# Down products of a SwiGLU layer by a two-by-two scheme with seven products, on one Trainium2 core

## Chip, core and metric

The kernel runs on one core of one Trainium2 chip. The metric is the time of the whole program on the device in microseconds; the time before is the median of three runs. One further run was profiled; its span is the time between the first and the last recorded instruction. TensorE is PE, VectorE DVE, ScalarE ACT, GpSimd POOL; SyncE (SP) issues nearly all transfers.

## What is computed

One transformer block on 2048 tokens of width 640 in f32: layer norm, attention with 32 heads of width 20, a projection and a residual sum, then layer norm, a SwiGLU layer of inner width 1728, and a residual sum. The change touches the last two lines.

```python
h = x + _A_ref(_layernorm(x), A_wqkv, A_wo)
def _B_ref(x, w_gate, w_up, w_down):
    g = _silu(x @ w_gate)
    u = x @ w_up
    return (g * u) @ w_down
h2 = h + _B_ref(_layernorm(h), B_w_gate, B_w_up, B_w_down)
```

## The kernel before

Every f32 product is made of three matmuls in the type fp32r: each operand is split into a high part (a copy, mostly on ACT) and a low part (the operand less its high part, on DVE or POOL; `split`, L75 to L77), and high by high, high by low and low by high are summed in PSUM.

**Attention.** Tokens come in four chunks of 512 (`CH`), 16 tiles of 128. After the projections for queries, keys and values, 32 units `u` (eight groups of four heads by four chunks) run over 16 key tiles `kt` each. `ORDER` spells the order in a key tile: scores (`s`, `S`), the maxima for coming units (`m`, `M`; `next_max`, `max_one`, L177 to L183), and once (`W`) the weighting of the values. When the last maximum of a unit is made, `max_all` (L187) reduces them on DVE and makes two small POOL instructions (L194, L195); two key tiles later `max_finish` (L199) transposes them on PE (L202). When a unit's sums are complete, ACT copies them out (L846).

**Weight preparation.** At `W`, one task of `prepare_weights` (L661) may be issued, except in unit 0, in key tiles 3 and 4, and where `max_all` just was (L927, L928). A block `f` of 128 inner columns (14 blocks, the last of 64) has the tasks load, nothing, two of sums, and eight that make one piece each; a piece is copied and subtracted on POOL (L676, L677) into a staging tile, of which there are four, and stored by the next task (L669) into `w_d`. Then `rows` (L740) does the same for the down weights, two blocks at a time: load, nothing, and four pieces (block by half of the 640 columns) into `d_d`. The tasks have to be through by unit 24, where the loads of `wo` begin.

**Feed-forward.** The chunks are taken in two pairs, `ELEMENTS` (L794) lists (pair, block) with the short block 13 first, and `e` is the place in this list. For a full block, `blocks` (L1103) makes gate and up for both chunks with seven products of 6 matmuls (128 x 512) and four of 3, in eight steps; what `done(0)` and `done(1)` receive, after steps' work 5 and 7, is the block's gated value for one chunk. For block 13 `plain` (L1082) has six steps. The PSUM banks `ps_a` (four) hold these products and `ps_b` (four) the down products. Weights come through rings (`Ring`, L771): eight places for units, three for lasts, four for halves of the down weights; `fill` loads the next ones at each step.

`parts` (L1029) splits the gated value. `to_come` (L1058) makes 16 pieces of it, each one `down` (L1039): for one token tile and one half, three matmuls of 128 x 320 (L1047; two in block 13, whose high and low parts share the rows) and one DVE addition to `h` (L1052). A block's pieces are issued in the next element's steps, so PE has them between its wide products. After block 12, the last of a pair, `out` is stored.

**Late tokens.** Pair 0 is normed and transposed before the feed-forward; pair 1 (chunks 2 and 3) during its first elements, by `late_tokens` (L1200): 15 small DVE items (`soon`, five a step), then 21 items (`late`, one a step), five for each token tile: for each of the two chunks a norm (L1216) and transposes on PE (L1232), split into the tile `kept` (two buffers) and stored into `z_d`; the sums of four blocks on POOL (L1249); and these split and stored into `t_d` (`store`, L1206). At e = 13 and 14 `swap` loads `z_d` and `t_d` over pair 0's operands (`SWAPS`, L1281). `step` (L1289) does all this in order: fills, swaps, down pieces, then a late item.

Of the kernel before, what the change touches and what calls it, by code (L numbers as in the profile page):

```python
# [43 lines left out]
def tile_block(ctx: ExitStack, tc: tile.TileContext, x, wqkv, wo, wg, wu, wd, out):  # L44
# [13 lines left out]
    d_d = [dram.tile([P, 2, 2 * HALF], F32R, name=f"d_d{f}") for f in range(NF)]  # L58
# [504 lines left out]
    wo_hi = pc.tile([P, ND, D], F32R, name="wo_hi", bufs=1)  # L563
    wo_lo = pc.tile([P, ND, D], F32R, name="wo_lo", bufs=1)
# [95 lines left out]

    def prepare_weights():  # L661
# [20 lines left out]
        def block(f):  # L682
# [33 lines left out]
            def unit(kind):  # L716
                store()
                t = staged([P, 2, 2, P])
                part(src[kind], t[:, 0], t[:, 1])
                stores.append((w_d[f][:, UNITS.index(kind)], t.rearrange("p i k n -> p (i k n)")))  # L720

            def last():
                store()
                t = staged([P, 2, 2, P])
# [7 lines left out]
            if not whole:  # L732
                return [load, nothing] + [lambda k=k: unit(k) for k in ("A11", "A12")] + [last]
            return (
                [load, nothing, lambda: sums(0), lambda: sums(1)]
# [4 lines left out]
        def rows(fs):  # L740

            raw = {}

            def load():
                store()
                for f in fs:
# [9 lines left out]
            def half(f, i):  # L756
                store()
                t = staged([P, 2, HALF])
                part(raw[f][:, i * HALF : (i + 1) * HALF], t[:, 0], t[:, 1])
                stores.append((d_d[f][:, i], t.rearrange("p i n -> p (i n)")))  # L760

            return [load, nothing] + [lambda f=f, i=i: half(f, i) for f in fs for i in range(2)]
# [4 lines left out]
        for f in range(0, NF, 2):  # L767
            tasks += rows((f, f + 1))
# [135 lines left out]
    for u in range(NU):  # L904
# [4 lines left out]
        for kt in range(NT):  # L909
# [49 lines left out]
            if kt in (12, 13) and 0 <= k + kt - 12 < ND:  # L959
                assert not preparing  # L960
                load_wo(k + kt - 12)
# [17 lines left out]
    for c in range(2, NC):  # L979
        h_c[c] = pe2.tile([P, TPC, D], F32, name=f"h{c}")  # L980
# [48 lines left out]
    def parts(f, s):  # L1029

        y_hi = pd2.tile([P, CH], F32R, name="y_hi", bufs=3)
        if f < NF - 1:
            y_lo = pd2.tile([P, CH], F32R, name="y_lo", bufs=3)
            split(s, y_hi, y_lo, nc.gpsimd)
            return y_hi, y_lo
        split(s[:LASTW], y_hi[:LASTW], y_hi[LASTW:], nc.gpsimd)
        return y_hi, None

    def down(c, t, half, d, y_hi, y_lo, final):  # L1039
        tt = c * TPC + t  # L1040
        pairs = [(y_hi, d[:, 0]), (y_hi, d[:, 1])]
        if y_lo is not None:
            pairs.append((y_lo, d[:, 0]))
        hs = slice(half * HALF, (half + 1) * HALF)
        ps = ps_b()
        for n, (a, b) in enumerate(pairs):
            nc.tensor.matmul(  # L1047
                ps[:, :HALF], a[:, t * P : (t + 1) * P], b,
                start=(n == 0), stop=(n == len(pairs) - 1),
            )  # L1050
        h = h_c[c][:, t, hs]
        nc.vector.tensor_tensor(out=h, in0=ps[:, :HALF], in1=h, op=ALU.add)  # L1052
        if final and half == 1:
            nc.sync.dma_start(out[tt * P : (tt + 1) * P, :], h_c[c][:, t, :])

    pending = []

    def to_come(pair, ys, final):  # L1058

        d = []  # L1060
        for i in range(2):
            for t in range(TPC):
                for half in range(2):
                    def piece(i=i, t=t, half=half):
                        if len(d) < 2:
# [282 lines left out]
```

## Time and profile before

| | |
|---|---|
| runs | 2137.73, 2142.70, 2144.39 us; median 2142.7 |
| profiled run | 2144.3 us; its span 2142.5 us |
| granted TensorE clock | 0.994 of full speed on the mean |
| DMA | 270.32 MB, mean 126 GB/s |
| down matmuls (L1047) | 896 + 416, DVE additions (L1052) 448 |
| loads | 186 units, 26 lasts, 56 halves |

A row of a timeline has the start and the length in us, engine, line, operation and operands; what stands in brackets is the idle time ahead of it and what ended that. A row of waits has the total, the times and the longest. Rows of the DMA queue have packets, MB and the share of the 16 engines' time in the stretch. Rows of the chain have start, length, and the number of instructions that were merged.

### The profile page before, as it was taken

How to read it: one execution, taken by the hardware profiler on the slowest of the kernel's cores; microseconds unless marked ns; L12 is line 12 of the kernel's file. 1: busy time of each engine (PE TensorE's matmuls, PEld its weight loads, DVE VectorE, ACT ScalarE, POOL GpSimd, SP SyncE). 2: the span in 40 equal slices, each digit the busy share in tenths (PEclk: the TensorE clock that was granted, in tenths of full speed). 3: DMA queues.
4: the chain of work that ended last, by engine and by line, in shares of the span. 5: the costliest groups of instructions: out<-in, count | busy, mean ns of one | idle time of the engine just before them, and what ended most of it. 6: DMA issues, size and time to landing. Idle time of an engine off the chain costs nothing.

```text
span 2142.5 us, 35011 instructions
## 1 busy us (share of the span) xinstructions
PE 2100.7 (98%) x12726; PEld 1224.7 (57%) x12726; DVE 1758.3 (82%) x2929; ACT 1281.1 (60%) x2491; POOL 495.0 (23%) x633
## 2 busy tenths in 40 slices
PE   7999999999999999999999999999999999999998
PEld 5766775333333333333333333335588888888887
DVE  6999996999889998999999999996367766666666
ACT  4222216999889998999999999996733211111111
POOL 5222212334343342410000010001145311111111
PEclk9999999999999999999999999999999999999999
DMA  7565532442533535522102113130238644764443
GB/s 249 158 189 172 159 107 81 120 150 94 161 115 104 172 100 154 185 92 56 48 22 77 30 46 92 26 109 22 71 112 256 211 133 146 276 228 145 131 143 108
DMA packets 203316, 270.32 MB, mean 126 GB/s; under 512 B 45624, under 2 KB 97848, under 8 KB 203144
## 3 DMA queue, kind: packets, MB, share of 16 engines
q1 hardware_dynamic: 189560, 241.86, 36.1%
q10 hardware_dynamic: 13584, 26.23, 4.0%
q8 instruction: 101, 1.65, 0.3%
q14 instruction: 71, 0.58, 0.1%
HBM read 182.68 MB, written 84.54 MB: 125 GB/s over the span
## 4 chain that ended last, share of the span: by engine, by line
PE 87%; DVE 6%; DMA 3%; POOL 2%; issue 2%; ACT 1%; SPq 0%; ACTq 0%; POOLq 0%; DVEq 0%
PE acc L836 23%; PE ps_a L993 14%; PE ps_max L177 14%; PE ps_one L826 14%; PE ps_b L1047 8%; PE ps_one L418 5%; DVE mx L171 3%; PE ps_one L452 2%; PE ps_wide L167 2%; PE ps_max L608 2%; PE ps_b L608 1%; DMA t_d<-kept 1%; DVE mx L183 1%; POOL zz L1249 0%; PE ps_one L386 0%
## 5 line engine op out<-in xcount | busy, mean ns | idle before, releaser
L832 ACT ACTIVATE probs<-ps_one 128x512 f32<-128x512 f32 x2048 | 1045.2, 621 | 137.0 <-PE ps_one L826 132.3
L183 DVE TENSOR_REDUCE mx<-ps_max 128x1 f32<-128x512 f32 x1632 | 1021.5, 683 | 108.2 <-PE ps_max L177 59.4
L826 PE MATMUL ps_one<-q_stk,k_stk 62*128 62x512 f32 x2048 | 552.2, 423 | 1.7 <-ACT probs L832 1.0
L836 PE MATMUL acc<-probs,v_stk 128*32 128x512 f32 x4096 | 547.9, 607 | 0.3
L177 PE MATMUL ps_max<-k_stk,q_stk 60*128 60x512 f32 x1632 | 544.1, 462 | 2.4 <-DVE mx L183 1.5
L177 PEld LDWEIGHTS ps_max<-k_stk,q_stk 60*128 60x128 f32 x1632 | 231.6, 185 | 431.7 <-DVE mx L183 411.3
L826 PEld LDWEIGHTS ps_one<-q_stk,k_stk 62*128 62x128 f32 x2048 | 300.7, 186 | 81.0 <-ACT probs L832 51.7
L171 DVE TENSOR_REDUCE mx<-ps_wide 128x2 f32<-128x1024 f32 x208 | 240.7, 1217 | 13.9 <-PE ps_wide L167 13.5
L1107 DVE TENSOR_TENSOR tmp<-ps_a,tmp 128x512 f32<-128x512 f32 x208 | 141.2, 689 | 125.7 <-PE ps_a L993 124.0
L1052 DVE TENSOR_TENSOR h<-ps_b,h 128x320 f32<-128x320 f32 x448 | 197.5, 483 | 11.5 <-PE ps_b L1047 11.5
L1047 PE MATMUL ps_b<-halves,y_hi 128*128 128x320 f32 x896 | 197.6, 309 | 0.2 <-DVE h L1052 0.2
L836 PEld LDWEIGHTS acc<-probs,v_stk 128*32 128x32 f32 x4096 | 80.9, 108 | 161.4 <-issue 152.7
L76 ACT ACTIVATE y_hi<-tmp 128x512 fp32r<-128x512 f32 (+1 forms) x56 | 35.3, 632 | 228.6 <-DVE tmp L1108 225.3
L1047 PEld LDWEIGHTS ps_b<-halves,y_hi 128*128 128x128 f32 x896 | 156.8, 188 | 20.7 <-DVE h L1052 2.0
L993 PE MATMUL ps_a<-t,units 128*128 128x512 f32 x624 | 162.8, 396 | 0.2 <-DVE kept L77 0.2
L77 POOL TENSOR_TENSOR y_lo<-tmp,y_hi 128x512 fp32r<-128x512 f32 x52 | 67.9, 1305 | 386.1 <-PE ps_a L993 241.9
L993 PE MATMUL ps_a<-z,units 128*128 128x512 f32 x516 | 133.7, 394 | 0.0
L1047 PE MATMUL ps_b<-halves,y_lo 128*128 128x320 f32 x416 | 127.5, 307 | 0.3 <-POOL y_lo L77 0.3
L993 PEld LDWEIGHTS ps_a<-t,units 128*128 128x128 f32 x624 | 112.5, 188 | 19.0 <-DVE kept L77 0.4
L194 POOL CAST both<-neg 128x16 fp32r<-128x16 f32 x32 | 6.6, 208 | 465.4 <-DVE neg L190 236.8
L993 PEld LDWEIGHTS ps_a<-z,units 128*128 128x128 f32 x516 | 93.1, 187 | 15.8
L993 PE MATMUL ps_a<-z,lasts 128*128 128x512 f32 x324 | 92.5, 393 | 0.2 <-DVE kept L77 0.2
(140 smaller groups left out, 1763.3 us busy)
## 6 DMA issues: line engine op xcount, KB each, us to landing
units<-w_d SPq DMA_DIRECT2D x186, 256.0 KB
w_d<-staged SPq DMA_DIRECT2D x106, 256.0 KB
halves<-d_d SPq DMA_DIRECT2D x56, 320.0 KB
raw<-qk_d SPq DMA_DIRECT2D x70, 160.0 KB
k_stk<-qk_d SPq DMA_DIRECT2D x64, 160.0 KB
q_stk<-qk_d SPq DMA_DIRECT2D x64, 160.0 KB
d_d<-staged SPq DMA_DIRECT2D x28, 320.0 KB
rb<-r_d SPq DMA_DIRECT2D x32, 256.0 KB
```

The costliest lines, as they stand in the source:

```text
L77: lo_engine.tensor_tensor(out=lo, in0=src, in1=hi.bitcast(F32), op=ALU.subtract)
L171: nc.vector.tensor_reduce(mx[:, :, pair, t, kc], ps, axis=AX.X, op=ALU.max)
L177: nc.tensor.matmul(ps, queries[u][rows, pair, t * P : (t + 1) * P], keys[u // NC][rows, pair, kc * CH : (kc + 1) * CH], start=True, stop=True,
L183: nc.vector.tensor_reduce(mxs[u][:, b, pair, t, kc : kc + 1], ps, axis=AX.X, op=ALU.max)
L418: nc.tensor.matmul(ps, w[:, k, m * P : (m + 1) * P], a[:, k, :], start=(n == 0 and k == 0), stop=(n == 2 and k == ND - 1),)
L826: nc.tensor.matmul(ps, keys[u // NC][rows, p, kt * P : (kt + 1) * P], queries[u][rows, p, :], start=True, stop=True,)
L832: nc.scalar.activation(probs[p][:, b, :], ps, AF.Exp, scale=scale)
L836: nc.tensor.matmul(acc[32 * j : 32 * j + 32, :], values[u // NC][:, kt, j * VW : j * VW + 32], probs[j // 2][:, j % 2, :], start=(kt == 0) ...
L993: nc.tensor.matmul(ps, w[k][:, i], z[k][:, j], start=(first and m == 0), stop=(last and m == len(n) - 1),)
L1047: nc.tensor.matmul(ps[:, :HALF], a[:, t * P : (t + 1) * P], b, start=(n == 0), stop=(n == len(pairs) - 1),)
L1052: nc.vector.tensor_tensor(out=h, in0=ps[:, :HALF], in1=h, op=ALU.add)
L1107: add = lambda out, ps, x: nc.vector.tensor_tensor(out=out, in0=ps, in1=x, op=ALU.add)
```

## The change

The down products of two neighbouring blocks (the inner dimension, 2 x 128) and two neighbouring token tiles (2 x 128), by the two halves of the 640 columns, are made with seven products for eight. The scheme needs four sums of the gated values (in a group, on POOL, `prepare`), four of the down weights (in the preparation, now stored as seven pieces in `j_d`), and sums of the products: three products are added to `h` directly, four into sums of their own, which `put_together` adds to `h` at a pair's end with eight POOL additions a group. Couples are joined in pair 0 for blocks 0 to 11, in pair 1 for 0 to 9; the others (`own`) go as before, in groups of two token tiles with four pieces.

The sums take the place of chunks 2 and 3 of `h`, which are stored to `h_d` in the late tokens and come back into the places of chunks 0 and 1 after pair 0's output (`bring_back`). The operands `yp` take the place of the late tokens' tiles: a joined group can only be prepared when `late` is through (`opened`); it has 17 items now, four for each token tile. `RATES` says how many pieces an element issues. The ring of halves has nine places. The gated value goes into a tile `y` (seven buffers). The preparation has ten staging places, two tiles of five, in the places of `wo_hi` and `wo_lo` (which are allocated later now), and one `nothing` more after each load. Of `soon`, seven items go with a step.

```diff
-        def staged(shape):
+        def staged(n):
             count[0] += 1
-            return pc.tile(shape, F32R, name="staged", tag=("o_hi", "o_lo")[count[0] % 2])
+            t = stages[count[0] % 2][:, count[0] // 2 % 5, : 2 * n]
+            return t.rearrange("p (i n) -> p i n", i=2), t
...
+            tasks = [load, nothing, nothing]
+            if together:
+                tasks += [lambda: sums(0), lambda: sums(1)]
+                for i, (_, name, _) in enumerate(SEVEN):
+                    tasks.append(lambda i=i, n=name: piece(n, j_d[fs[0] // 2][:, i]))
+            else:
+                for f in fs:
+                    for i in range(2):
+                        tasks.append(lambda f=f, i=i: piece((f, i), d_d[f - NF + 4][:, i]))
...
+    SEVEN = (
+        ("A11", "B11", 0), ("S2", "T2", 1), ("S3", "T3", 2), ("S1", "T1", 3),
+        ("A12", "B21", (0, 0)), ("S4", "B22", (0, 1)), ("A22", "T4", (1, 0)),
+    )
+    def own(pair, f):
+        return f >= (NF - 2, NF - 4)[pair]
...
+        def prepare(self):
+            if self.parts is not None or not (pools or self.fs[0] == NF - 1):
+                return
...
+            p = self.parts = pools[0].tile([P, 2, 7, P], F32R, name="yp", tag="yp", bufs=3)
...
+            a, b = self.ys
+            split(cols(b, t, 2), p[:, 0, 1:3], p[:, 1, 1:3], nc.gpsimd)
+            x = tmp().rearrange("p (k n) -> p k n", k=4)
+            a11, a21, a12 = cols(a, t)[:, 0], cols(a, t + 1)[:, 0], cols(b, t)[:, 0]
+            tt = nc.gpsimd.tensor_tensor
+            tt(out=x[:, 0], in0=a21, in1=cols(b, t + 1)[:, 0], op=ALU.add)
+            tt(out=x[:, 1], in0=x[:, 0], in1=a11, op=ALU.subtract)
+            tt(out=x[:, 2], in0=a11, in1=a21, op=ALU.subtract)
+            tt(out=x[:, 3], in0=a12, in1=x[:, 1], op=ALU.subtract)
+            split(cols(a, t), p[:, 0, :1], p[:, 1, :1], nc.gpsimd)
+            split(x, p[:, 0, 3:], p[:, 1, 3:], nc.gpsimd)
...
+        def seven(self, n):
+            name, _, place = SEVEN[n]
+            if self.tp == 0:
+                self.d.append(down_ring.take())
+            d, k = self.d[n], SLOTS.index(name)
+            y_hi, y_lo = self.parts[:, 0, k], self.parts[:, 1, k]
+            ps = self.multiply([(y_hi, d[:, 0]), (y_hi, d[:, 1]), (y_lo, d[:, 0])])
+            if self.tp == 3:
+                down_ring.free()
+            if isinstance(place, tuple):
+                self.add(ps, *place)
+            else:
+                own_sum = sums[self.tp][place]
+                if self.fs[0] == 0:
+                    nc.vector.tensor_copy(own_sum, ps)
+                else:
+                    nc.vector.tensor_tensor(out=own_sum, in0=ps, in1=own_sum, op=ALU.add)
+            if n == 6 and own(self.pair, self.fs[1] + 1):
+                self.put_together()
...
+    def prepare_some():
+        for g in waiting[:2]:
+            g.prepare()
...
             z = zs[c, t] = pl.tile([P, D], F32, name="z3", bufs=2)
...
+            stores.append((h_d[c - 2, :, t], h_c[c][:, t, :]))
...
-            items.append(lambda t=t: keep_sums(0, t))
-            items.append(lambda t=t: (store(), keep_sums(1, t)))
+            items.append(lambda t=t: (keep_sums(0, t), keep_sums(1, t)))
...
+    RATES = {
+        1: (6, 2), 2: (10, 0), 3: (4, 7), 4: (17, 0), 14: (12, 0), 15: (16, 0), 16: (16, 0),
+        25: (18, 0), 26: (22, 0), 27: (26, 0),
+    }
...
+    def bring_back():
+        for c, t in again:
+            nc.sync.dma_start(h_c[c][:, t, :], h_d[c, :, t])
+            h_c[c + 2] = h_c[c]
+        again[:] = stored
+        stored.clear()
...
+        number, begin = RATES.get(e, (14 if e else 0, 0))
+        each = spread_over(number, steps, begin)
...
             for _ in range(each[n]):
-                if old:
-                    old.pop(0)()
+                next_down()
+            if not late and e > 2:
+                prepare_some()
+            for _ in range(2):
+                if chores:
+                    chores.pop(0)[2]()
...
             elif late:
                 late.pop(0)()
+                if not late:
+                    pl_ctx.close()
+                    opened()
```

More of the change, by code (lines that the diff above doesn't have):

```diff
@@ L732, in block @@
             if not whole:
-                return [load, nothing] + [lambda k=k: unit(k) for k in ("A11", "A12")] + [last]
+                return [load, nothing, nothing] + [lambda k=k: unit(k) for k in ("A11", "A12")] + [last]
             return (
-                [load, nothing, lambda: sums(0), lambda: sums(1)]
+                [load, nothing, nothing, lambda: sums(0), lambda: sums(1)]
                 + [lambda k=k: unit(k) for k in ("A11", "A12")] + [last]
@@ L1027, in quarter_sums @@
         ]
[L1029 to L1065, printed above, removed]
-                            d.append(down_ring.take())
-                        down(2 * pair + i, t, half, d[half], *ys[i], final)
-                        if (i, t) == (1, TPC - 1):
-                            down_ring.free()
-                    pending.append(piece)
+    def own(pair, f):
+        return f >= (NF - 2, NF - 4)[pair]
@@ L1072, in bank, with next_down, to_come @@
+    def prepare_some():
+        for g in waiting[:2]:
+            g.prepare()
+    def next_down():
+        if not waiting:
+            return
+        g = waiting[0]
+        prepare_some()
+        f, i = g.steps.pop(0)
+        f(i)
+        if not g.steps:
+            waiting.pop(0)
+    def to_come(i, pair, fs, ys, d):
+        waiting.extend(Group(pair, tp, fs, ys, d) for tp in (2 * i, 2 * i + 1))
     def bank():
@@ L1317, in tile_block @@
             (plain if f == NF - 1 else blocks)(step, done)
-        to_come(pair, ys, f == NF - 2)
-    for f in pending:
-        f()
+        before = ys
+    while waiting:
+        next_down()
 _INS = ["A_x", "A_wqkv", "A_wo", "B_w_gate", "B_w_up", "B_w_down"]
```

186 lines of the change are left out of this document (149 added, 37 removed).

## The prediction

> **What bounds the kernel now.** I read the busy shares on the profile's page first, then the busy times by stretch, then the chain that ended last.
>
> ```profile
> PE 2100.7 (98%) x12726; PEld 1224.7 (57%) x12726; DVE 1758.3 (82%) x2929; ACT 1281.1 (60%) x2491; POOL 495.0 (23%) x633
> ```
> ```profile
> 1600.00:1700.00 100.00, 97.52 (x516) 83.78 (x516) 74.76 (x155) 29.88 (x58) 47.13 (x43) 1.00 0.77 237
> 1700.00:1800.00 100.00, 100.00 (x522) 87.45 (x521) 68.00 (x134) 15.66 (x25) 12.98 (x10) 1.00 0.43 141
> ```
>
> The columns of a stretch are PE, PEld, DVE, ACT and POOL busy, granted clock, DMA share and GB/s. From 1670 us on, PE never rests until the tail, the other engines have room, and DMA is under half used: there, a matmul less is its time less. Between 1600 and 1670 PE loses 2.5 us and DMA is at 0.77 and more; that stretch decides this case.
>
> The chain between 1700 and 1800 us is PE alone and gives the price of a matmul:
>
> ```profile
> 1707.59 1.39 PE ps_a L993 x6
> 1708.98 0.88 PE ps_b L1047 x6
> ...
> 1712.13 2.09 PE ps_a L993 x9
> ...
> 1727.14 1.39 PE ps_a L993 x6
> ```
>
> Six down matmuls take 0.875 us, 0.146 each; a 512-wide one takes 0.2325 (2.09 / 9). One block of 54 wide and 48 down matmuls takes 19.55 us (1727.14 - 1707.59).
>
> **The change, part by part.** The profiled run is 2144.3 us, its span 2142.5; the median of the runs is 2142.7, 1.6 below the profiled run. I work on the span.
>
> *1. Matmuls removed.* Pair 0 joins f = 0 to 11 (6 couples), pair 1 f = 0 to 9 (5). Each couple has 4 groups of two token tiles, each group 7 products for 8, each product 3 matmuls: 11 x 4 x 3 = 132 matmuls of 0.146 us: **-19.3 us**, if PE stays full. DVE has 28 adds for 32 in a couple, and no new kind but a copy: nothing.
>
> *2. Weight preparation.* Before: 13 x 12 + 5 + 7 x 6 + 1 = 204 tasks, one for a key tile at most. After: 13 x 13 + 6 + 6 x 12 + 2 x 7 + 1 = 262; it ends some 4.5 units later, still ahead of the loads of wo. PE mostly does not feel these tasks, but three times it does:
>
> ```profile
> 453.44 0.62 ACT L846 ACTIVATE o<-acc 128x512 f32<-128x512 f32 x1
> ...
> 562.70 0.61 ACT L846 ACTIVATE o<-acc 128x512 f32<-128x512 f32 x1
> 600.72 0.63 ACT L846 ACTIVATE o<-acc 128x512 f32<-128x512 f32 x1
> ...
> 680.18 0.62 ACT L846 ACTIVATE o<-acc 128x512 f32<-128x512 f32 x1
> ...
> 789.25 0.62 ACT L846 ACTIVATE o<-acc 128x512 f32<-128x512 f32 x1
> ...
> 902.09 0.62 ACT L846 ACTIVATE o<-acc 128x512 f32<-128x512 f32 x1
> ```
> ```profile
> PE ps_one L202 <- POOL both L195: 7.6, 3, 4.1
> ```
> ```profile
> 611.89 0.42 SPq L696 DMA_DIRECT2D raw<-in_B_w_gate  x1
> ```
> ```profile
> 621.01 0.72 POOL L708 TENSOR_TENSOR sums<-raw 128x256 f32<-128x256 f32 x1 [21.20 <-DMA raw<-in_B_w_up]
> ```
> ```profile
> 610.00:640.00 30.00, 25.82 (x168) 0.89 0.40 124
> ```
>
> L846 ends a unit; from 453.44 to 562.70, to 680.18, to 789.25 and to 902.09 it is three units each: 109.3, 117.5, 109.1 and 112.8 us. The second and fourth are 8.2 and 3.7 long: **11.9 us** lost. The mechanism: POOL, in order, stands at L708 until a load lands 9 us after its issue; behind it wait the small casts of max_all (L194, L195), and for these the transposes of max_finish, so PE sits for 7.6 us in three waits, and its clock falls for a while (0.89). Counting the tasks against the units, these are just the three units where max_all follows the first task that needs a load (sums(0), or the first half) within a key tile. After the change each load has one key tile more (36.4 / 16 = 2.3 us), and that task falls within one key tile of max_all only at units 3, 4 and 19. Of these only unit 4 has its load issued late, three key tiles ahead (6.8 us), like the mildest of today's three, whose unit (562.70 to 600.72, 38.0 us) is 1.6 us over a third of 109.3; I leave it 2 us. Ten staging places take POOL's waits for stores away too. I take **-10 us**, with ends 0 (the stalls come back elsewhere) and -12. The Trainium skill, "TensorE: Matmul & The Clock Gate", Part 1, says that an idle window of about 3.4 us halves PE's clock until it has been busy as long; the 4.1 us wait with 0.89 after it agrees, and by that rule an idle PE costs more than its idle time, which speaks against part 3 below.
>
> *3. The late tokens.* This is what the change puts at risk. late_tokens writes chunks 2 and 3 out; its 17 items now have to be through by step 3 of e = 3, where pl closes, and a joined group can't be prepared before. What they store goes up by h_d, and what PE has to do meanwhile goes down: steps of e = 1 to 3 issue 6, 10 and 4 down pieces, 16 of them of two matmuls, and the rest of the down work comes later.
>
> ```profile
> 1602.77 1.56 PE L993 MATMUL ps_a<-z,units 128*128 128x512 f32 x6
> ...
> 1624.28 0.71 PE L1232 MATMUL ps_a<-ident,z 128*128 128x128 f32 x5
> 1624.74 1.65 PE L993 MATMUL ps_a<-t,units 128*128 128x512 f32 x6
> ```
> ```profile
> q1 hardware_dynamic: 14691, 28.11, 42.8%
> ```
> ```profile
> q1 hardware_dynamic: 15567, 11.33, 94.9%
> ...
> units<-w_d SPq DMA_DIRECT2D x13, 256.0 KB
> z_d<-kept SPq DMA_DIRECT2D x6, 512.0 KB
> t_d<-kept SPq DMA_DIRECT2D x4, 512.0 KB
> halves<-d_d SPq DMA_DIRECT2D x4, 320.0 KB
> z_d<-kept SPq DMA_DIRECT2D x6, 128.0 KB
> lasts<-w_d SPq DMA_DIRECT2D x1, 256.0 KB
> ```
> ```profile
> 1631.69 0.64 ACT L76 ACTIVATE kept<-zz 128x512 fp32r<-128x512 f32 x1 [4.53 <-DMA t_d<-kept]
> ```
> ```profile
> 1626.39 0.53 SPq L1206 DMA_DIRECT2D t_d<-kept  x1
> ...
> 1670.91 0.53 SPq L1206 DMA_DIRECT2D t_d<-kept  x1
> ```
>
> PE alone would need 3 x 54 x 0.2325 + 32 x 0.146 + 8 flips x 0.46 = 46 us from 1602.8, and stand at the first joined piece at 1649. DMA needs longer. From 1900 to 2100 us the queue moved 28.11 MB of loads at a share of 42.8%, thus 328 GB/s when at work. From 1630 to 1670 it was at 94.9%; its loads (4.98 MB) take 15.2 of these 38.0 us at that rate, which leaves 22.8 us for 6.03 MB of z_d and t_d: 264 GB/s. After the change there must pass from 1603 on: z_d and t_d 9.43 MB, 35.7 us; h_d eight of 0.328 MB, 8.0; nine halves, filled at once, 9.0; 19 units and 3 lasts, 17.6: **70 us**, until 1673. The stores are in the way of the engines: kept has two buffers, ACT waits for a store before it writes the next (the row of 4.53 us), and behind it wait the copies and Silus that free PE's banks. The last three of the four token tiles take 14.8 us each today (1626.39 to 1670.91, the first t_d of each), in five items, nearly all of it DMA; with four items a tile moves as many bytes (h_d in place of a unit and the halves), so it takes no less. I put the first joined piece at 1678: 1673 and 5 us for the last landing and the operands.
>
> ```profile
> 1670.00:1680.00 10.00, 10.00 (x53) 8.51 (x52) 7.70 (x15) 2.39 (x4) 3.67 (x3) 1.00 0.89 269
> ```
>
> PE is full from 1670, so its third block ends two blocks ahead of 1707.59, at 1668.5, and by then 32 more full pieces are done, 32 x 0.4375 = 14.0 us. So the stretch costs 1678 - 1668.5 + 14.0 = **+23.5 us**. The ends: -5.5 (PE alone, 1649) and +30 (a few us of DMA idle in the first 20).
>
> *4. Operands of the joined groups.* For each group POOL does one subtraction of 256 columns, one of 128, one of 512 and four additions of 128.
>
> ```profile
> 723.59 0.73 POOL L677 TENSOR_TENSOR staged<-raw,staged 128x256 fp32r<-128x256 f32 x1
> ...
> 724.63 0.46 POOL L677 TENSOR_TENSOR staged<-raw,staged 128x128 fp32r<-128x128 f32 x1
> ...
> 823.07 0.88 POOL L677 TENSOR_TENSOR staged<-raw,staged 128x320 fp32r<-128x320 f32 x1
> ...
> 1619.54 1.29 POOL L77 TENSOR_TENSOR y_lo<-tmp,y_hi 128x512 fp32r<-128x512 f32 x1 [1.41 <-ACT y_hi L76]
> ```
>
> 0.73 + 5 x 0.46 + 1.29 = 4.3 us; 44 groups, 190 us in some 440. They are made a group ahead, four steps or some 9 us, which hides them; ACT waits inside for POOL, 2.6 us (0.73 + 4 x 0.46), with p1's copy behind it on ACT and DVE's adds behind that, and PE's four banks cover it. I take 0; without the cover each group would wait a part of it, at 0.5 us 44 x 0.5 = **22 us**. The 64 put_together additions of 0.88 us run two a step on POOL: 1.8 us of a step of 2.4, with the operands beside them in e = 14: 0 to +3. The store of out waits for them on SP, and behind it the ring loads, eight units ahead: nothing.
>
> *5. More loads.* 89 halves come in for 56; eight h_d loads come at e = 15 and 16. At e = 13 they meet the swaps:
>
> ```profile
> q1 hardware_dynamic: 7171, 17.91, 95.9%
> ```
>
> That is 1845 to 1895 us, full as it is; some 1.6 MB more, 5 us of queue, against a ring nine deep: 0 to +5, I take **+1**.
>
> The sum: 2142.5 - 19.3 - 10 + 23.5 + 1 = 2137.7; with the 1.8 us around the span 2139.5, and on the median's scale **2138 us**.
>
> **Rivals.**
> *The late stretch drains faster (B).* Items come closer together, the queue has more to choose from, and py's places may come free before the last store. Against it: 0.95 was the share with the queue crowded. For it: z_d and t_d at the 328 GB/s of the loads would end all after 63 us, at 1666, the first piece at 1668: 10 less, **2128 us**. The Trainium skill, "DMA: Bandwidth & Descriptors", Specifications, gives about 358 GB/s for a core's HBM traffic and full rate from 512 bytes on; by an estimate from that the 20.8 MB take 58 us. The trace disagrees: 264 in the crowded stretch.
> *The preparation's stalls stay (C).* For it: three chances in 20 units. Then -10 falls away: **2148 us**.
> *Operands late, slower than before (D).* PE waits at joined groups because ACT and POOL are asked in one order: 0.5 us for each of 44 groups, **2160 us**. It beats the gain from 0.11 us a group on ((2142.7 - 2138) / 44). Against it: POOL at 13% of the steady stretch. That slices of a staging tile are followed as one, so that ten places act as two, would end on this side too; the rings of units, sliced alike, speak against it.
>
> **How the numbers follow.** About 0.3% (6.4 us) is what a measurement of this kernel can tell from no change: faster below 2136.3, slower above 2149.1. Forecast A (2131 to 2146) 0.45, B 0.25, C 0.14, D 0.16. Faster: B and 0.4 of A, 0.43; same: the rest of A and most of C, 0.37; slower: D and some of C, 0.20. The range 2123 to 2156 leaves out the lower edge of B and half of D.
>
> **What would show it.** Down matmuls 1180 for 1312; waits of L202 for POOL below 3 us in all; PE idle by 25 us or more between 1600 and 1680, with DMA share above 0.9 there and ACT waiting for z_d, t_d or h_d; after it PE at 100% again, with blocks of 18.7 us (19.55 - 6 x 0.146) on average. I am wrong if PE is full in the late stretch, or idle by more than 5 us behind it.

## The result, and the profile after

The changed kernel takes 2154.66 us (median of 5 runs, 2153.15 to 2159.55), the kernel before 2142.70 (5 runs, 2137.73 to 2148.88): a ratio of 1.0058, 95% interval 1.0035 to 1.0081. It is slower, by 12 us or 0.6%. The prediction had 2138, with 0.43 for faster and 0.2 for slower; the time is inside its range (2123 to 2156), the direction is not the one it held likeliest.

The profiled execution is the 2154.66 one, its span 2152.9 us. Its busy shares, from the page:

```profile
PE 2092.1 (97%) x12594; PEld 1213.1 (56%) x12594; DVE 1739.1 (81%) x2885; ACT 1302.5 (60%) x2587; POOL 729.0 (34%) x1037
```

PE issues 132 matmuls fewer (12726 before) and is busy 8.6 us less, although those matmuls were worth 19.3 us; and it rests more, since the span grew. The busy times of two stretches say where, in the columns of the prediction:

```profile
1600.00:1700.00 100.00, 77.73 (x337) 62.91 (x336) 50.05 (x100) 26.98 (x57) 51.09 (x63) 0.86 0.74 238
1700.00:1800.00 100.00, 100.00 (x516) 87.03 (x515) 66.26 (x129) 21.58 (x48) 46.94 (x75) 1.00 0.56 182
```

From 1700 PE is as full as before. Between 1600 and 1700 it lost 2.5 us before and loses 22.3 now, and its granted clock is 0.86 for 1.00, so even what it counts as busy is partly slow work. The waits of PE, longest sums first (total, times, longest):

```profile
PE ps_a L1374 <- ACT zz L1379: 10.4, 3, 4.5
...
PE ps_b L1123 <- ACT yp L78: 5.6, 1, 5.6
PE ps_b L1123 <- DMA halves<-j_d: 4.2, 3, 2.7
...
PE ps_one L868 <- ACT probs L874: 3.2, 1, 3.2
...
PE ps_b L1123 <- POOL yp L79: 2.8, 3, 1.9
...
PE ps_b L1123 <- DVE own L1144: 1.8, 1, 1.8
...
PE ps_one L204 <- POOL both L197: 0.2, 1, 0.2
```

L1374 is the transpose of a late token (L1232 before), L1123 a down matmul, L868 the scores, L204 the transpose of `max_finish`. The last row is the gain: the 7.6 us of the preparation's stalls have become 0.2. The first row was 1.2 us before and the fourth 1.0; the second and third are new.

**A ledger by stages.** Four moments are found in every profile: the end of the unit near 450 us (ACT's copy of its sums), the last `max_finish`, the first product of the feed-forward behind the projections, and the end. In the kernel before the first three are at 453.44, 1493.28 and 1602.77; in the changed one:

```profile
451.01 0.62 ACT L888 ACTIVATE o<-acc 128x512 f32<-128x512 f32 x1
```
```profile
1479.77 0.28 PE L204 MATMUL ps_one<-ident,both 128*32 128x128 f32 x1 [0.16 <-POOL both L197]
...
1595.57 1.57 PE L1038 MATMUL ps_a<-z,units 128*128 128x512 f32 x6
```

The same four moments, read in the same way in each profile of this study (us; the kernels are introduced below):

| kernel | start to unit | unit to last max_finish | to feed-forward | feed-forward |
|---|---|---|---|---|
| before | 453.44 | 1039.84 | 109.49 | 539.7 |
| changed | 451.01 | 1028.76 | 115.80 | 557.3 |
| e3_preparation | 455.15 | 1029.29 | 109.59 | 540.7 |
| e1_no_store | 450.36 | 1028.73 | 112.81 | 552.8 |
| e5_21_items | 453.17 | 1028.68 | 113.30 | 555.3 |
| e7_busy | 446.71 | 1028.86 | 112.46 | 557.2 |
| e6_halves_ahead | 455.09 | 1028.82 | 112.43 | 555.3 |
| e10_split_later | 455.89 | 1028.97 | 109.78 | 558.9 |
| e4_fill | 455.89 | 1028.52 | 114.04 | 526.7 |
| e8_part_later | 448.16 | 1028.92 | 109.88 | 526.6 |
| e9_early_store | 457.73 | 1028.99 | 111.71 | 525.8 |
| e11_both | 452.91 | 1028.89 | 107.14 | 528.4 |

The first column is scatter: it runs from 446.7 to 457.7 with no regard to the edit, and it is most of what makes one profiled execution differ from another. The second repeats within 0.8 us in the eleven kernels with the new preparation, the fourth within some 2 us between like kernels. The third is less steady. e1, e5, e6 and e7 have the code of the changed kernel up to the feed-forward, and in this stage they take 112.4 to 113.3 us, where the changed kernel's profiled execution takes 115.8. Still, a stage tells more than a span. Changed less before: -2.4 (scatter), -11.1 (preparation), +6.3 (a wait that the prediction had not counted; +2.9 to +3.8 in those four), +17.6 (feed-forward): +10.4, the difference of the spans.

Inside the feed-forward I go by the starts of the gated products on DVE (of each element the second), and by 0.146 us for a down matmul:

- +30.3 up to e = 5, all that the late stretch costs. Its product starts 122.4 us behind the first product of the feed-forward, for 104.8 before, and by then 87 down matmuls fewer have been issued, which is 12.7 us of work put off. Two other kernels with the same code up to there, e6 and e10, have 28.7 and 29.6.
- -19.3 for the 132 matmuls that are gone.
- +7.7 at the swaps: from the product of e = 12 to that of e = 16 it takes 77.0 us for 70.3, with 7 matmuls fewer.
- -1.1 for the rest.

### The profile page after: what moved, and what is told of

It reads as the page before. It is cut to its first block, busy times and chain, and to the rows that moved or that the text cites. A ratio compares the mean times of both kernels' runs of the same rounds, so it can differ in the third digit from the quotient of the medians.

```text
span 2152.9 us, 35419 instructions
## 1 busy us (share of the span) xinstructions
PE 2092.1 (97%) x12594; PEld 1213.1 (56%) x12594; DVE 1739.1 (81%) x2885; ACT 1302.5 (60%) x2587; POOL 729.0 (34%) x1037
## 4 chain that ended last, share of the span: by engine, by line
PE 85%; DMA 5%; DVE 4%; POOL 3%; ACT 1%; issue 1%; SPq 0%; ACTq 0%; POOLq 0%; DVEq 0%
PE acc L878 23%; PE ps_max L179 15%; PE ps_one L868 14%; PE ps_a L1038 13%; PE ps_b L1123 7%; PE ps_one L420 5%; DVE mx L173 3%; PE ps_wide L169 2%; PE ps_one L454 2%; PE ps_max L611 2%; DMA z_d<-kept 1%; DMA halves<-j_d 1%; PE ps_b L611 1%; DMA t_d<-kept 1%; DMA o_t<-o_d 1%
## 5 line engine op out<-in xcount | busy, mean ns | idle before, releaser
L868 PE MATMUL ps_one<-q_stk,k_stk 62*128 62x512 f32 x2048 | 550.5, 421 | 3.9 <-ACT probs L874 3.2
L868 PEld LDWEIGHTS ps_one<-q_stk,k_stk 62*128 62x128 f32 x2048 | 299.8, 185 | 84.1 <-ACT probs L874 55.1
L1123 PE MATMUL ps_b<-halves,yp 128*128 128x320 f32 x1116 | 197.5, 312 | 15.2 <-ACT yp L78 5.6
L1123 PEld LDWEIGHTS ps_b<-halves,yp 128*128 128x128 f32 x1116 | 180.1, 190 | 35.3 <-issue 7.1
L79 POOL TENSOR_TENSOR yp<-y,yp 128x256 fp32r<-128x256 f32 x104 | 65.0, 625 | 198.2 <-ACT yp L78 198.1
L1128 DVE TENSOR_TENSOR h<-ps_b,h 128x320 f32<-128x320 f32 x228 | 103.4, 482 | 8.0 <-PE ps_b L1123 7.0
L1285 ACT ACTIVATE tmp<-tmp 128x512 f32<-128x512 f32 x26 | 16.4, 632 | 147.7 <-DVE tmp L1240 147.6
L78 ACT ACTIVATE yp<-tmp 128x512 fp32r<-128x512 f32 x44 | 27.8, 632 | 121.3 <-POOL tmp L1116 121.3
```

What stands on the lines that cost most here:

```text
L79: lo_engine.tensor_tensor(out=lo, in0=src, in1=hi.bitcast(F32), op=ALU.subtract)
L868: nc.tensor.matmul(ps, keys[u // NC][rows, p, kt * P : (kt + 1) * P], queries[u][rows, p, :], start=True, stop=True,)
L1123: nc.tensor.matmul(ps, a, b, start=(n == 0), stop=(n == len(pairs) - 1))
L1128: nc.vector.tensor_tensor(out=h, in0=ps, in1=h, op=ALU.add)
```

## The experiments

Each kernel was timed in several rounds beside the kernel before. The theory: the preparation gains its 10 us, the late stretch gives them back and more, because the queue has h_d to carry and PE has no down work to cover it with. The rivals: it is the number of items, or the lowered clock behind each wait.

**The preparation alone.** The kernel before with ten staging places and the second `nothing`, the rest untouched:

```diff
-    wo_hi = pc.tile([P, ND, D], F32R, name="wo_hi", bufs=1)
-    wo_lo = pc.tile([P, ND, D], F32R, name="wo_lo", bufs=1)
+    stages = [
+        pc.tile([P, 5, 2 * HALF], F32R, name="stage", tag=tag, bufs=1) for tag in ("wo_hi", "wo_lo")
+    ]
...
-            return [load, nothing] + [lambda f=f, i=i: half(f, i) for f in fs for i in range(2)]
+            return [load, nothing, nothing] + [lambda f=f, i=i: half(f, i) for f in fs for i in range(2)]
```

> The kernel before with ten staging places and one task more after each load, and nothing else of the change. Theory (POOL standing at a late load made PE wait three times): no wait of L202 for POOL above 0.5 us, the last max_finish 12 to 14 us earlier. If the 3.2 us wait at the last unit's end, with the slow clock behind it, was a matter of how transfers fell in that run, total 2129 to 2132 us; if it belongs to the changed preparation, 2134 to 2137. Rival (the preparation's stalls were a matter of chance): 2140 to 2146.

2136.4 us, a ratio of 0.996 (0.9944 to 0.9976): faster than the kernel before. Ahead of 1460 us PE waits for POOL's `both` once; the two moments in its profile follow.

```profile
PE ps_one L202 <- POOL both L195: 0.5, 1, 0.5
```
```profile
1484.44 0.28 PE L202 MATMUL ps_one<-ident,both 128*32 128x128 f32 x1 [0.15 <-POOL both L195]
...
1594.03 1.57 PE L999 MATMUL ps_a<-z,units 128*128 128x512 f32 x6
```

The second stage is 1029.3 us for 1039.8, the others as before. Part 2 of the change is worth 10.5 us by itself, a little less than expected, and what makes the whole slower lies elsewhere. The time is the one expected if the wait at the last unit's end came with the new preparation, but the profile says otherwise: PE waits 0.7 us for the probs there, so the staging alone does not bring it.

**No stores of h.** The eight stores of `h_d` go, and `x` is read back where `h_d` was:

```diff
-            stores.append((h_d[c - 2, :, t], h_c[c][:, t, :]))
...
-            nc.sync.dma_start(h_c[c][:, t, :], h_d[c, :, t])
+            tt = (c + 2) * TPC + t
+            nc.sync.dma_start(h_c[c][:, t, :], x[tt * P : (tt + 1) * P, :])
```

> Leaves out the eight stores to h_d; what comes back for chunks 2 and 3 is the input x, so the residual of the attention is missing in half the output. Theory (the late stretch is held by the bytes that the queue has to move): 2.62 MB less at 328 GB/s, the first joined piece 8 us earlier, some 65 us behind the first block's first matmul where it was 73.5; total 2145 to 2148 us. Rival (it is held by the order of the items on ACT and POOL with two buffers of kept, whatever the bytes): first joined piece within 2 us of 73.5, total 2153 to 2156.

2147.7 us, 1.0014 (1.0002 to 1.0025). On PE, the start of the feed-forward and the first joined piece:

```profile
1591.90 1.56 PE L1038 MATMUL ps_a<-z,units 128*128 128x512 f32 x6
...
1660.82 0.87 PE L1123 MATMUL ps_b<-halves,yp 128*128 128x320 f32 x2 [5.16 <-ACT yp L78]
```

That is 68.9 us behind, where the changed kernel has 73.55; the feed-forward is 4.5 us shorter, and the waits of the transposes for `zz` fall from 10.4 to 5.2 us. So the stores do lie on the path, but for 4.5 of the 8 us that the prediction gave their bytes in the queue: the result lies between what the theory and the rival expected.

**More items.** The last item of a token tile is cut in two again, 21 items as before the change, with the joined groups from e = 4 on:

```diff
-            items.append(lambda t=t: (keep_sums(0, t), keep_sums(1, t)))
+            items.append(lambda t=t: keep_sums(0, t))
+            items.append(lambda t=t: (store(), keep_sums(1, t)))
...
-        1: (6, 2), 2: (10, 0), 3: (4, 7), 4: (17, 0), 14: (12, 0), 15: (16, 0), 16: (16, 0),
+        1: (6, 2), 2: (10, 0), 3: (0, 0), 4: (21, 0), 14: (12, 0), 15: (16, 0), 16: (16, 0),
```

> The change with 21 late items as before, the first joined pieces at e = 4. Theory (bytes): the last t_d store lands when it did, within 3 us, PE idle as much, total 2151 to 2158 us. Rival (four items a tile crowd POOL and ACT, and PE waits for them): the late waits of PE fall by half, total 2140 to 2147.

2152.23 us, 1.0038 (1.0025 to 1.0052).

```profile
1595.15 1.56 PE L1038 MATMUL ps_a<-z,units 128*128 128x512 f32 x6
...
1670.10 0.87 PE L1123 MATMUL ps_b<-halves,yp 128*128 128x320 f32 x2 [11.24 <-DMA units<-w_d]
```

The first joined piece is 74.95 us behind, 1.4 later than in the changed kernel, with more items and a wait twice as long just ahead of it: the waits moved, and their sum between 1590 and 1700 us is 23.9 for 22.1 (the rows of the view of waits added up). How the work is cut into items isn't what sets the time of the first joined piece.

**PE kept busy.** Matmuls whose result nobody reads, in the places of the five longest waits:

```diff
+    def busy(n):
+        if n:
+            ps = ps_b()
+        for m in range(n):
+            nc.tensor.matmul(ps, t14[:, 0, 0, :P], t14[:, 0, 1], start=(m == 0), stop=(m == n - 1))
...
+        if (g.pair, g.tp, g.fs) == (0, 0, (0, 1)):
+            busy({7: 24, 6: 8}.get(len(g.steps), 0))
...
             for k in range(ND):
+                if c == 3 and k == 4:
+                    busy((0, 16, 12, 10)[t])
```

> The changed kernel with matmuls added whose result nobody reads, 128 x 512 into a bank of their own: 16, 12 and 10 ahead of the fifth transpose of chunk 3's tiles 1 to 3, 24 ahead of the first joined piece and 8 ahead of the second. They fill the waits of 4.5, 3.4, 2.5, 5.6 and 1.9 us after which the six matmuls of a product took 2.93 us in place of 1.56. Theory (the halved clock behind a wait is part of the loss, about 10 us of longer matmuls in all, 3.6 of them behind the first joined piece, where nothing hides them): the groups of six behind these places take 1.6 us or less, the granted clock is above 0.95 from 1600 to 1690, and the time is 2 to 5 us less, 2150 to 2153. Stronger form (PE's late transposes are themselves what delays the stores): 8 us or more less, 2147. Rival (DMA alone sets the stretch): no change within 1.5 us, or later by what the added matmuls overrun.

2157.59 us (2146.97 to 2164.85), 1.0055 (1.0035 to 1.0076). First a piece of the changed kernel, then the same place here:

```profile
1614.67 0.66 PE L1374 MATMUL ps_a<-ident,z 128*128 128x128 f32 x4
1619.85 0.48 PE L1374 MATMUL ps_a<-ident,z 128*128 128x128 f32 x1 [4.52 <-ACT zz L1379]
1620.34 2.93 PE L1038 MATMUL ps_a<-t,units 128*128 128x512 f32 x6
```
```profile
1588.03 1.55 PE L1038 MATMUL ps_a<-z,units 128*128 128x512 f32 x6
...
1607.53 3.90 PE L1195 MATMUL ps_b<-t 128*128 128x512 f32 x16
1612.37 0.33 PE L1384 MATMUL ps_a<-ident,z 128*128 128x128 f32 x1 [0.94 <-ACT zz L1389]
1612.86 1.67 PE L1038 MATMUL ps_a<-t,units 128*128 128x512 f32 x6 [0.16 <-DVE kept L79]
...
1661.13 0.53 PE L1123 MATMUL ps_b<-halves,yp 128*128 128x320 f32 x2 [1.96 <-ACT yp L78]
```

The edit did to the clock what it should: the six matmuls behind the wait take 1.67 us for 2.93. It did nothing to the time: the first joined piece comes 73.1 us behind the start, for 73.55, and the feed-forward takes 557.2 us for 557.3. Where PE waits for something that comes later anyhow, its slow work costs nothing. The theory of the clock falls, in both its forms, for all that lies ahead of the first joined piece. Behind it the added matmuls overran what they were to cure (eight took 3.44 us, at a granted clock of 0.53 themselves), so there the run decides nothing. The profiled execution is also the fastest of the eight, and its first stage, 446.71 us, is the shortest of all profiles here; where the slower ones lose, up to 2164.85 us, no profile shows.

**Halves ahead of the swaps.** Elements 12 and 13 issue 21 and 7 pieces for 14 and 14:

```diff
-        1: (6, 2), 2: (10, 0), 3: (4, 7), 4: (17, 0), 14: (12, 0), 15: (16, 0), 16: (16, 0),
+        1: (6, 2), 2: (10, 0), 3: (4, 7), 4: (17, 0), 12: (21, 0), 13: (7, 0), 14: (12, 0), 15: (16, 0), 16: (16, 0),
```

> The changed kernel, but the down pieces of elements 12 and 13 are issued 21 and 7 where each issued 14, so that the first group of the next couple, and with it the loads of its seven halves, starts an element ahead of the swaps. Theory (step 5 was mis-sized: behind the swaps' 1 MB loads the halves land late, 4.2 us of waits and about 6 us in all between 1860 and 1910): the three waits of the down matmuls (L1123) for halves go, and the time falls by 3 to 6 us, to 2149 to 2152. Rival (the bytes are too many for that stretch, whatever their order): PE waits for the halves in e = 12 or for z and t instead, 3 us or more, and the time stays at 2154 +- 1.5.

2151.89 us, 1.0038 (1.0025 to 1.0051). The busy times around the swap in the changed kernel, then the wait that is left in this one behind 1700 us:

```profile
1850.00:1860.00 10.00, 10.00 (x54) 8.74 (x53) 5.63 (x12) 2.89 (x6) 5.63 (x12) 1.00 0.80 262
1860.00:1870.00 10.00, 7.18 (x33) 5.14 (x31) 6.09 (x12) 1.57 (x4) 4.07 (x7) 1.00 1.03 405
1870.00:1880.00 10.00, 8.41 (x44) 7.37 (x45) 4.36 (x9) 1.11 (x3) 6.46 (x7) 1.00 1.04 393
1880.00:1890.00 10.00, 9.27 (x50) 7.99 (x49) 4.90 (x12) 3.46 (x8) 8.91 (x13) 1.00 0.86 327
```
```profile
PE ps_a L1038 <- DMA z<-z_d: 3.7, 2, 3.5
```

The three waits for halves are gone and one of 3.5 us for `z` stands in their place, with PE's clock at 0.71 behind it; from the gated product of e = 5 to that of e = 16 it takes 207.2 us for 207.6. The median is 2.8 us lower than the changed kernel's and lies where the theory had it, but the intervals overlap, and of the 2.0 us by which the feed-forward is shorter 1.6 lie ahead of e = 5, where this edit does nothing. By the stretch itself the rival is right: the queue is full there, and another order only chooses who waits.

**The wait for o_t.** The one wait that no part of the prediction had was looked for on ACT. The row of the changed kernel:

```profile
1492.06 0.74 ACT L78 ACTIVATE o_hi<-o_t 128x640 fp32r<-128x640 f32 x1 [3.53 <-DMA o_t<-o_d]
```

ACT, in order, stands at a split for the projection; behind it the probs, for which PE waits 3.2 us. In the kernel before the same place costs 1.0 us. I first moved the wrong split, that of projection(2), in the version e4_fill (told below):

```diff
-                if NT - 4 <= kt < NT - 1:
+                if kt == NT - 1 and c == NC - 1:
+                    ahead[0][2]()
+                if NT - 4 <= kt < NT - (2 if c == NC - 1 else 1):
                     ahead[0][kt - NT + 4]()
```

> The version with the first couple unjoined (e4_fill), with the split of the first o_t of the last projection but one issued one key tile later, behind the last probs. Theory (ACT stood in front of the probs for a load of o_t, 2.9 us at the last weighting, and gave away a part of what the preparation gained): the wait for probs goes, 0 to 1 us appears at the projection's first matmul, and the time is 1.5 to 3.5 us under e4_fill's 2123.3, at 2120 to 2122. Rival (the projection then waits as long): 2123 +- 1.

2122.28 us, 0.9896 (0.987 to 0.9923), against e4_fill's 0.9901. The wait of L868 stayed, 2.2 us, since its load belongs to projection(1); yet the stage is 4.2 us shorter, a little more than the 3.4 by which it scatters between the changed kernel and its four likes. The edit's own part is small: the waits of the last projection's matmuls for its split, 1.1 us in e4_fill, are gone. More of it is in what follows the wait of L868, here e4_fill, then this kernel:

```profile
1497.67 1.95 PE L868 MATMUL ps_one<-q_stk,k_stk 62*128 62x512 f32 x4 [2.93 <-ACT probs L874]
1499.56 1.86 PE L878 MATMUL acc<-probs,v_stk 128*32 128x512 f32 x8
1501.35 1.70 PE L611 MATMUL ps_max<-wo_hi,o_hi 128*128 128x320 f32 x5
```
```profile
1489.64 1.96 PE L868 MATMUL ps_one<-q_stk,k_stk 62*128 62x512 f32 x4 [2.23 <-DMA h<-in_A_x]
1491.53 1.06 PE L878 MATMUL acc<-probs,v_stk 128*32 128x512 f32 x8
1492.53 1.00 PE L611 MATMUL ps_max<-wo_hi,o_hi 128*128 128x320 f32 x5
```

Behind 2.93 us the next matmuls take 1.86 and 1.70 us, behind 2.23 us 1.06 and 1.00: here, where nothing hides it, a slower clock does cost. (The granted clock is 0.51 in the one case, from 1499.6 to 1503.0, and 1.00 in the other, from 1491.6 to 1493.6.) Then the right split, in the changed kernel alone: the same edit with `c == 2` for `c == NC - 1`.

> The changed kernel, with only the first split of projection(1) (its o_t, L78 and L79) issued one key tile later, behind the probs for which the last weighting waited; e8_part_later had moved the split of the wrong projection, and the wait of 2.2 to 3.2 us had stayed. Theory (ACT stands in front of the probs for the load of o_t, and the matmuls behind the wait run at a lowered clock): the wait of L868 for probs falls below 0.7 us, the stretch from the last max_finish to the start of the feed-forward falls from 115.8 us to 109.5 to 111.5, as before, and the time by 3 to 6 us to 2149 to 2152. Rival (the projection's own first matmuls then wait as long): the stretch stays at 113 to 116 us.

2150.49 us, 1.0025 (1.001 to 1.004).

```profile
1484.86 0.28 PE L204 MATMUL ps_one<-ident,both 128*32 128x128 f32 x1 [0.15 <-POOL both L197]
...
1497.78 1.00 PE L611 MATMUL ps_max<-wo_hi,o_hi 128*128 128x320 f32 x5 [0.67 <-ACT o_hi L78]
...
1594.64 1.55 PE L1040 MATMUL ps_a<-z,units 128*128 128x512 f32 x6
```

The wait for probs is gone, 0.67 us stands at the projection, and the stage takes 109.8 us for 115.8, as the theory had it. Against the four kernels with the same code up to there (112.4 to 113.3), though, the gain is 2.6 to 3.5 us and not 6.0. The median is 4 us lower, its interval overlapping that of the changed kernel a little. That the wait goes is shown; what it is worth lies between 2.6 and 6.0 us.

**The stretch filled.** Pair 0's blocks 0 and 1 are not joined; their pieces need no `yp` and go into the late stretch, 16, 13 and 13 of them in e = 1 to 3. Ten couples are joined for eleven, which gives 12 of the 132 matmuls back.

```diff
+    def early(pair, f):
+
+        return pair == 0 and f < 2
     def own(pair, f):
 
-        return f >= (NF - 2, NF - 4)[pair]
+        return f >= (NF - 2, NF - 4)[pair] or early(pair, f)
...
-        1: (6, 2), 2: (10, 0), 3: (4, 7), 4: (17, 0), 14: (12, 0), 15: (16, 0), 16: (16, 0),
-        25: (18, 0), 26: (22, 0), 27: (26, 0),
+        1: (16, 2), 2: (13, 0), 3: (13, 0), 4: (6, 0), 14: (12, 0), 15: (16, 0), 16: (16, 0),
+        25: (16, 0), 26: (20, 0), 27: (23, 0),
...
+            if early(pair, f):
+                y_hi, y_lo = (pd2.tile([P, CH], F32R, name="y", tag="y", bufs=7) for _ in range(2))
+                split(s, y_hi, y_lo, nc.gpsimd)
+                ys[i] = y_hi, y_lo
```

> The change, but blocks 0 and 1 of pair 0 stay unjoined with operands made at once, so that PE has 48 pieces for the late stretch, and the late items are 21 again. Theory (PE is idle there because its work was put off while the bytes stayed): matmul saving 17.5 us for 19.3, the stretch at most 8 us longer than before the change, no wait at the first joined piece, and no slow clock; total 2120 to 2130 us. Rival (joined groups cost PE time all along, or the operands for them): no better than 2145.

2123.26 us, 0.9901 (0.988 to 0.9922): about 20 us faster than the kernel before and 31 than the changed one.

```profile
1600.00:1700.00 100.00, 95.17 (x484) 81.34 (x483) 70.57 (x144) 29.91 (x62) 56.17 (x63) 0.98 0.87 283
```
```profile
PE ps_a L1384 <- ACT zz L1389: 4.2, 2, 3.0
```

PE loses 4.8 us in the stretch for 22.3, with DMA busier than ever (0.87): the transfers are all still there, and PE has something to do. The feed-forward is 30.7 us shorter. As a couple now begins an element later than before, the halves also come ahead of the swaps, and no wait for them is left. The terms of the ledger tell the two apart. Up to e = 5 the cost is +3.0 us for +30.3 (the product comes 99.9 us behind the start, with 54 down matmuls fewer than before the change), and at the swaps it is +2.3 for +7.7 (70.5 us, with 14 fewer). So some 27 us come from the late stretch and 5 from the swaps, and the 12 matmuls take 1.75 back.

**Chunk 2's stores earlier.** e8_part_later, and in it four of the eight stores of `h_d` during the last projection:

```diff
         if i % 2 == 0:
             quarters.pop(0)()
+            nc.sync.dma_start(h_d[0, :, i // 2], h_c[2][:, i // 2, :])
...
-            stores.append((h_d[c - 2, :, t], h_c[c][:, t, :]))
+            if c == 3:
+                stores.append((h_d[c - 2, :, t], h_c[c][:, t, :]))
```

> The kernel of e8_part_later, and in it the four stores of chunk 2's h are issued during the last projection, where DMA is at a share of 0.1 to 0.3, rather than among the late tokens. Theory (every store among the late tokens costs its queue time, 1 us for 0.328 MB; eight of them cost 4.6 us in e1_no_store): the waits of the flips (4.2 us) and of z fall by half, 1 to 3 us less than e8_part_later. Rival (with the plain down pieces as cover the stores are hidden): the same within 1 us.

2124.64 us, 0.9901 (0.988 to 0.9922): no gain. The feed-forward is 0.9 us shorter and the stage ahead of it 1.8 longer, both within the scatter of these stages. With PE covered, the stores that cost 4.5 us in the changed kernel cost nothing worth moving.

**Both edits.** e4_fill with the first splits of projection(1) and projection(2) a key tile later (`c >= 2` in the edit above):

> The version with the first couple unjoined (e4_fill), with the first splits of projection(1) and projection(2) both one key tile later. Theory: the stretch from the last max_finish to the feed-forward takes 109 to 110.5 us in place of 114.0, the rest 526.5 us as in e4_fill and e8_part_later, the time 2118 to 2121. Rival: 2123 +- 1.

2120.78 us (2113.22 to 2124.11), 0.9875 (0.9849 to 0.9902), the lowest median of this study, though its interval overlaps those of e4_fill and e8_part_later. The stage ahead of the feed-forward takes 107.1 us, and L868 no longer waits for probs; the feed-forward's 528.4 gives 1.7 of it back.

## Why the prediction was wrong, by its steps

*Part 1, the matmuls.* Right. 132 are gone, and behind e = 5 the blocks follow each other in 18.67 us (seven from 1717.94 to 1848.61, by the gated products on DVE) where they took 19.55; 6 x 0.146 had given 18.67.

*Part 2, the preparation.* Right in mechanism and size: -11.1 us for -10, the waits of L204 down to 0.2, and -10.5 when made alone. What the sum lacked is a wait at its far end, which it put at nothing. ACT's split for projection(1) sits ahead of the probs, and its load lands later than before: +6.3 us in the profiled execution, +2.9 to +3.8 in four kernels with the same code there, and all but 0.3 gone in e10_split_later. The prediction had asked what would be late next when a stall goes, but only inside the preparation.

*Part 3, the late tokens.* This is the step that failed, as a size: +30.3 us for +23.5, the price put on the stretch, at the upper end of +30 that the prediction allowed. The time of its end was well met: the queue was named as the limit, and the first joined piece came 73.55 us behind the start, for 75.2. What was missed stands behind that piece:

```profile
1668.41 0.61 ACT L78 ACTIVATE yp<-y 128x256 fp32r<-128x256 f32 x2 [5.43 <-DMA t_d<-kept]
```
```profile
1669.12 0.87 PE L1123 MATMUL ps_b<-halves,yp 128*128 128x320 f32 x2 [5.62 <-ACT yp L78]
1671.86 1.17 PE L1123 MATMUL ps_b<-halves,yp 128*128 128x320 f32 x3 [1.87 <-POOL yp L79]
1673.46 2.23 PE L1123 MATMUL ps_b<-halves,yp 128*128 128x320 f32 x7 [0.43 <-POOL yp L79]
1675.50 1.62 PE L1038 MATMUL ps_a<-z,units 128*128 128x512 f32 x6
1678.90 1.89 PE L1123 MATMUL ps_b<-halves,yp 128*128 128x320 f32 x6 [1.78 <-DVE own L1144]
```

ACT makes the first operands only when the last store of `t_d` has left the memory that they take. Then the first groups have no cover: the second piece waits 1.87 us for the operands that POOL makes one after another, twelve matmuls (1.75 us at 0.146) fill the 6.4 us until 1675.50, which is 4.6 lost. In e = 4 a wait for the first copies into the new sums and slow matmuls cost 3.7 more (it takes 23.7 us, and its 54 wide and 51 down matmuls are worth 20.0). 4.6 and 3.7, less the 1.65 by which the first piece was early, are 6.65 of the 6.8 us that were missing. The prediction had worked out what a group's operands cost (4.3 us) and hidden them a group ahead; the first groups have no group ahead of them. Two of the prediction's signs were missed by a little: between 1600 and 1680 us PE idles 22.3 us for the 25 named, a part of the loss being slow work (granted clock 0.84) and not rest, and DMA's share there is 0.86 for 0.9 (0.92 from 1595 to 1669).

The Trainium skill, "TensorE: Matmul & The Clock Gate", Part 1, was cited against part 3: an idle PE costs more than its idle time. The trace agrees with the mechanism (2.93 us for 1.56 behind the wait of 4.52), but e7_busy shows that ahead of the first joined piece it had no price. "DMA: Bandwidth & Descriptors", Specifications, was cited as the ground of rival B, by an estimate of 58 us for the bytes. The trace doesn't bear it out: the stretch took 73.55, and from 1596 to 1670 DMA moved 299 GB/s on the mean, not 358.

*Part 4, the operands.* Right: from 1700 to 1800 PE is 100% busy with POOL at 47%, and rival D has no wait to show but 0.5 us.

*Part 5, the loads.* The second size that failed: +7.7 us for +1, above its upper end of 5. The bytes were counted, and the queue known to be full; that PE would wait for them was put at nearly nothing because of a ring nine places deep. But a couple takes seven of the nine at once, and by the reading of the code two places ahead don't outlast a queue that is full for 20 us; no run had a deeper ring. e6_halves_ahead shows that the order isn't the cause; why e4_fill has only 2.0 us of waits there and e6_halves_ahead 3.7 stays open.

*The rivals.* B had the trace against it, C fell with part 2, D with part 4: it alone had the sign, for a reason that the profile doesn't show. The kernel is slower because the forecast's own loss in part 3 was some 7 us larger, the swaps cost some 7 us more than put, and the wait for o_t, 3 to 6 us, wasn't put at all. The test of the prediction, "I am wrong if PE is ... idle by more than 5 us behind it", did catch the swaps: 5.1 us of idle time between 1860 and 1890.

What stays open: why the load of `o_t` takes 5.6 us from issue to landing in the changed kernel and 3.8 before, though its neighbours on the queue are the same, and why e3_preparation, with the same staging, doesn't have the wait. What is shown is only that the wait can be had back.

## What to carry to other kernels

When a change puts work off, look at the stretch that it is taken from: if a transfer sets that stretch, the work was its cover, and the part that is put off is paid in full, with the first instructions behind it that have no predecessor to hide their operands. Leaving the change out of just that stretch cost 12 of 132 matmuls here and turned 12 us of loss into some 20 us of gain. And compare two profiles by stages between moments that both have, since the difference of two spans here holds up to 11 us of scatter from the first 450 us alone.

## What the hardware showed

The clock behind a wait doesn't go by its length alone. Waits of 2.93 us (e4_fill, above) and 2.54 us (the changed kernel, below) were followed by slow matmuls, at a granted clock of 0.51 and 0.50; one of 2.69 us (below) and one of 2.23 us (e8_part_later, above) were not, the clock staying at 1.00:

```profile
1648.79 0.47 PE L1374 MATMUL ps_a<-ident,z 128*128 128x128 f32 x1 [2.54 <-ACT zz L1379]
1649.28 2.93 PE L1038 MATMUL ps_a<-t,units 128*128 128x512 f32 x6
...
1871.43 0.68 PE L1123 MATMUL ps_b<-halves,yp 128*128 128x320 f32 x3 [2.69 <-DMA halves<-j_d]
...
1872.78 1.55 PE L1038 MATMUL ps_a<-z,units 128*128 128x512 f32 x6
```

Six matmuls of the same shape take 2.93 us in the one case and 1.55 in the other. The Trainium skill, "TensorE: Matmul & The Clock Gate", Part 1, says that the window of some 3.4 us in which the activity is judged runs freely. If so, it matters where a wait falls in it, and these rows fit that. The same part has the clock fall after at least one idle window of some 3.4 us; here the waits of 2.54 and 2.93 us were shorter and the clock was halved all the same, so the measurement decides: a wait needn't be 3.4 us long to have its price.

The same bytes can take the queue different times. Two stretches of the changed kernel moved 22.12 MB each, 1596 to 1670 us (late tokens, 74 us) and 1820 to 1900 us (swaps, 80 us); packets, MB and share:

```profile
q1 hardware_dynamic: 25087, 22.12, 93.2%
...
q1 hardware_dynamic: 9302, 22.12, 77.6%
```

In the first they took 69.0 us of the queue (0.932 x 74), in packets of some 880 bytes on the mean; in the second 62.1 us, in packets of 2.4 KB; and in the two fullest windows at the swap the queue moved 405 and 393 GB/s, more than the 328 that the prediction took for loads.
